# Half of the first 1024 tokens of x turned on TensorE instead of by transposing loads

## The chip, the cores and the metric

The kernel runs on one core of one Trainium2 chip. The metric is device time in microseconds. The kernel before took 833.27 us (median of 4 runs, 832.85 to 833.89). One execution was profiled; it took 833.1 us, and its trace spans 831.4 us from the first to the last instruction, so 1.7 us of it lie outside the trace.

## The reference, cut to what matters

The input x has 2048 tokens of 512 bf16 values. Two blocks work on the same x and are mixed token by token:

```python
g = sigmoid((x * gate_w).sum(-1))
q, k, v = split(x @ wqkv)                 # 32 heads of 16 columns each
o = softmax(q @ k.T / 4) @ v              # per head, 2048 x 2048 scores
a = o @ wo
b = (silu(x @ w_gate) * (x @ w_up)) @ w_down   # hidden width 1792
out = g * a + (1 - g) * b
```

Most of the work is the exponential of 32 x 2048 x 2048 scores.

## The kernel before, in words

**Tiling.** The tokens lie in 4 query blocks of 512 (QBW) and 16 key tiles of 128 (KT). Four heads form a group, and there are 8 groups. A unit is one query block with one group; there are 32 units, each with 16 key tiles. The order of units (UNIT, line 115) takes group 0 of all four query blocks first. For each unit and key tile TensorE makes four score tiles of 128 x 512. Two of them share one PSUM tile `s_t`, and ScalarE turns it into `e_t` with one exponential of 128 x 1024 (`emit_pair`, line 709). Some key tiles go to VectorE instead: `emit_d` (line 742) makes the scores one at a time in `d_t`, and VectorE builds the exponential in steps (`y_t`, `z_t`, `u_t`), with one accumulating DMA from GpSimd's queue (line 789) and a last VectorE step when that has landed (`last`, line 792). Both kinds are then multiplied with V on TensorE (`o_ps`, line 876).

**Order.** The order of instructions on each engine is fixed when the program is built. `ordered` (line 146) chains every TensorE, ScalarE, VectorE and SP-queue instruction issued after it is defined to the one before on its engine. A planner (`Plan`, line 281, and the loop at line 1372) keeps model clocks `plan.pe`, `plan.dve` and `plan.act` and decides from them which piece comes next: a score pair, a score tile for VectorE, a product with V, or a piece of a side chain. Side chains (projections, gate, feed-forward) have a release slot and a due slot. A change of one model clock at the start can therefore move any later instruction, although none is added or dropped.

**Transposed input.** Every projection needs x with its 512 columns on the partitions. The tile is `xT[128, 4, 2048]`: index `dc` says which 128 columns. Lines 177 to 179 fill it with eight transposing loads on SP's queue, four (`dc` 0 to 3) for tokens 0 to 1023 and then four for tokens 1024 to 2047. Behind them on the same queue stand the rest of the V weights (line 190, tile `rb`), the rest of the Q and K weights (line 192), `gw_col`, `wo_t` and `wo_l`. ScalarE's queue loads the 64 columns of K, Q and V that group 0 needs (lines 183 and 188).

**Start.** VectorE clears small tiles, copies the K and then the Q columns of group 0 into padded weights `wpad` (line 234), and writes ones into `kaug` for groups 1 to 3 (`ones_rows`, lines 237 to 241). GpSimd clears and fills constants; `ident`, the identity matrix, is made at lines 268 to 271. TensorE runs 14 matmuls on zeros (`keep_warm`, line 996), and then for each `dc` two matmuls into `kp0` (K of the first 1024 tokens), one into `qp0` (Q of the first 512), and two more on zeros between (lines 1019 to 1026). After these come, in order: the largest magnitude of K on VectorE (`largest`), the bound `kneg1`, its product on TensorE (`bound_add`), the two query variants `q0a` on VectorE (line 1034), and with them the first scores and the first exponential. ScalarE writes `kaug` for group 0 from `kp0` (line 1030) and evicts V of group 0 (`v0`, line 454). VectorE then writes ones for group 4 (line 1037). Line 1045 sets the planner's VectorE clock to `plan.pe + 3.0`. K of the second 1024 tokens follows as side chains (`k0_pieces`, line 1052), with the bounds over all keys (`bound_all`, line 1063) and the query block computed again (`again`, line 1091).

**End.** After the last exponential TensorE adds up the last output projections. `tail` (line 969) issues the five matmuls of each of two row blocks, one group of five before the last product with V (line 1434) and one after it (line 1452). Then follow the copy `osb`, the denominators (`dt`, `rt`, `rps`), the scaling `on_l`, four matmuls, four evictions and the stores (lines 1453 to 1477).

**Tiles that are shared.** `wd_t` (line 198) holds the feed-forward's last weights later; until they are loaded, from slot 88 on (line 1264), VectorE uses its first four rows as a work buffer (line 765). `ps_s` has two PSUM tiles of two banks for `kp0` and the `s_t`; `ps_m` has three single banks, handed out by `m_tile` (line 340).

Of the kernel before, what the change touches and what calls it, by code (L numbers as in the profile page):

```python
# [8 lines left out]
ACT = mybir.ActivationFunctionType  # L9
ALU = mybir.AluOpType  # L10
AX = mybir.AxisListType
BF16 = mybir.dt.bfloat16
F32 = mybir.dt.float32
# [66 lines left out]
def kernel(  # L80
# [12 lines left out]
    nc = tc.nc  # L93
    P = 128
    x = A_x.flatten_outer_dims()
    S, D = x.shape
# [5 lines left out]
    DC = D // P  # L102
    FC = F // P
    KT = S // P
    QBW = 512
    QB = S // QBW
    TQ = QBW // P
# [23 lines left out]
    const = ctx.enter_context(tc.tile_pool(name="const", bufs=1))  # L131
    big = ctx.enter_context(tc.tile_pool(name="big", bufs=1))
# [6 lines left out]
    ps_s = ctx.enter_context(tc.tile_pool(name="ps_s", bufs=2, space=bass.MemoryType.PSUM))  # L139
# [6 lines left out]
    def ordered(ins):  # L146
        i = ins.ins
        if i.engine in last_of:
            tc.add_manual_dep(
                i, last_of[i.engine].name,  # L150
                mybir.DependencyInfo(mybir.DependencyClass.NoSync, mybir.DependencyReason.DATA),
                reason="order",
            )
        last_of[i.engine] = i
        return ins

    def mm(*args, **kw):
        return ordered(nc.tensor.matmul(*args, **kw))  # L158

    def act(*args, **kw):  # L160
        ordered(nc.scalar.activation(*args, **kw))  # L161
# [10 lines left out]
    vec = Ordered(nc.vector)  # L172
    queue = Ordered(nc.sync)


    xT = big.tile([P, DC, S], BF16, name="xT")
    for t0 in (0, 2 * QBW):
        for dc in range(DC):
            queue.dma_start_transpose(out=xT[:, dc, t0:t0 + 2 * QBW], in_=x[t0:t0 + 2 * QBW, dc * P:(dc + 1) * P])
    wqk = big.tile([P, DC, 2 * D], BF16, name="wqk")  # L180
    for c0 in (D, 0):

        nc.scalar.dma_start(out=wqk[:, :, c0:c0 + 64],
                            in_=A_wqkv[:, c0:c0 + 64].rearrange("(dc p) c -> p dc c", p=P))

    rb = big.tile([P, NB, QBW], BF16, name="rb")
    wv = rb[:, :, :]
    nc.scalar.dma_start(out=wv[:, :, 0:64], in_=A_wqkv[:, 2 * D:2 * D + 64].rearrange("(dc p) c -> p dc c", p=P))
# [2 lines left out]
    for c0 in (D, 0):  # L191
        queue.dma_start(out=wqk[:, :, c0 + 64:c0 + D],
                          in_=A_wqkv[:, c0 + 64:c0 + D].rearrange("(dc p) c -> p dc c", p=P))
# [1 line left out]
    wo_t = big.tile([P, NB, D], BF16, name="wo_t")  # L195

    wo_l = big.tile([P, 2, D], BF16, name="wo_l")
    wd_t = big.tile([P, FC, D], BF16, name="wd_t")

    def late_loads():  # L200
        queue.dma_start(out=gw_col[:], in_=gate_w.rearrange("(dc p) -> p dc", p=P))
# [10 lines left out]
    kaug = big.tile([P, G, S], BF16, name="kaug")  # L212
# [4 lines left out]
    wpad = [mt[:, i, :].rearrange("p (dc c) -> p dc c", c=P) for i in range(2)]  # L217
# [12 lines left out]
    nc.vector.memset(bsel0, 0.0)  # L230
    for j in range(4):
        nc.vector.memset(bsel0[32 * j:32 * j + 32, 32 * j:32 * j + 1], -1.0)
    for i in (1, 0):
        nc.vector.tensor_copy(
            out=wpad[i][:, :, :].rearrange("p dc (j c) -> p dc j c", c=32)[:, :, :, 1:1 + DH],
            in_=wqk[:, :, i * D:i * D + 64].rearrange("p dc (j c) -> p dc j c", c=DH))
    def ones_rows(engine, g):

        engine.memset(kaug[:, g, :].bitcast(F32), 1.0019378662109375)
    for g in range(1, 4):  # L240
        ones_rows(nc.vector, g)
    vaug = big.tile([P, KT, G * 4 * VC + 16], BF16, name="vaug")
    nc.gpsimd.memset(vaug[:, :, G * 4 * VC:], 0.0)

# [20 lines left out]
    nc.gpsimd.memset(sel_t[:], 0.0)  # L265
    for j in range(4):
        nc.gpsimd.memset(sel_t[32 * j:32 * j + 1, j:j + 1], 1.0)
    ident = const.tile([P, P], BF16, name="ident")
    nc.gpsimd.memset(ident[:], 1.0)
    nc.gpsimd.affine_select(out=ident[:], in_=ident[:], pattern=[[-1, P]], compare_op=ALU.is_equal,  # L270
                            fill=0.0, base=0, channel_multiplier=1)

    kb = const.tile([P, NB], F32, name="kb")
    kneg = const.tile([P, NB, 8], BF16, name="kneg")
# [13 lines left out]
    plan = Plan()  # L288
# [38 lines left out]
    def m_ready(n=1):  # L327

        t = sorted(b for b in banks if b is not None)
        return t[n - 1] if len(t) >= n else None  # L330

    def stuck():
        if d_wait:
            pay_d()
        elif owed:
            pay()
        else:
            emit_piece(pace.cur)

    def m_tile(name):  # L340
        while m_ready() is None:
            stuck()
        i = min((i for i in range(3) if banks[i] is not None), key=lambda i: banks[i])
        plan.pe = max(plan.pe, banks[i])
        banks[i] = None
        held[i] = ps_m[i].tile([P, QBW], F32, tag=f"m{i}", name=name)
        return held[i]

    def m_free(ps, t):
        i = [h is ps for h in held].index(True)  # L350
        banks[i], held[i] = t + 0.2, None
# [152 lines left out]
    for g in range(5, G):  # L504
        ones_rows(nc.gpsimd, g)
# [487 lines left out]
    qp0 = m_tile("qp0")  # L993
    warm = ps_o.tile([P, QBW], F32, tag="o", name="warm")

    def keep_warm(n):
        for _ in range(n):
            mm(warm[:, :], lhsT=idle[:, 0:P], rhs=idle[:, :], start=True, stop=True)
# [14 lines left out]
    def largest(i, ps):  # L1013
        vec.tensor_reduce(out=kpart0[:, i:i + 1], in_=ps, axis=AX.X, op=ALU.max, apply_absolute_value=True)
# [1 line left out]
    def k_neg(to, i, before):  # L1016
        vec.scalar_tensor_tensor(out=to, in0=bsel0, scalar=kpart0[:, i:i + 1], in1=before, op0=ALU.mult, op1=ALU.min)

    keep_warm(14)
    for dc in range(DC):  # L1020
        for tb in range(2):
            mm(kp0[:, tb * QBW:(tb + 1) * QBW], lhsT=wpad[1][:, dc, :], rhs=xT[:, dc, tb * QBW:(tb + 1) * QBW],
               start=(dc == 0), stop=(dc == DC - 1))
        mm(qp0[:, :], lhsT=wpad[0][:, dc, :], rhs=xT[:, dc, 0:QBW], start=(dc == 0), stop=(dc == DC - 1))
        if dc < DC - 1:
            keep_warm(2)
    largest(0, kp0[:, :])
    k_neg(kneg1, 0, idle[:, 0:P])
    act(out=aq0, in_=qp0[:, :], func=ACT.Abs)
# [4 lines left out]
        vec.tensor_scalar(out=q0a[:, v, :], in0=qp0[:, :], scalar1=vsel[:, v:v + 1], scalar2=None, op0=ALU.mult)  # L1034
    vec.tensor_copy(out=q0_bf[0], in_=qp0[:, :])
    m_free(qp0, plan.pe + 2.0)
    ones_rows(vec, 4)

    vec.tensor_scalar(out=lo_t[:], in0=lo_t[:], scalar1=pidx[:, 0:1], scalar2=None, op0=ALU.subtract)
    vec.tensor_scalar(out=far_t[:], in0=lo_t[:], scalar1=-float(DH) + 0.5, scalar2=-1.0,  # L1040
# [1 line left out]
    vec.scalar_tensor_tensor(out=bsel[:, :], in0=lo_t[:], scalar=0.5, in1=far_t[:],  # L1042
                                   op0=ALU.is_lt, op1=ALU.mult)
    plan.act = plan.pe
    plan.dve = plan.pe + 3.0


    pace = Pacer()
# [60 lines left out]
    for qb in range(1, QB):  # L1109
        d = qb * KT  # L1110
# [5 lines left out]
    for qb in range(QB):  # L1116
        for b in range(NB):
            d = UNIT.index((qb, max(2 * b, 1))) * KT
# [253 lines left out]
    while au < UNITS:  # L1372
# [10 lines left out]
        if room > 0.02:  # L1383
# [19 lines left out]
            if room > 0.4 and closed in o_of and 0 < pvs[closed] < KT - 1 and (closed or pvs[0] != KT // 2) and sum(  # L1403
                    w for t, w in work_at[-24:] if t > plan.pe - 3.0) < 6.5:

                for j in range(4):
                    mm(o_of[closed][32 * j:32 * j + 16, :], lhsT=vaug[:, 0, G * 4 * VC:], rhs=xT[:, 0, 0:QBW],
                       start=False, stop=False, tile_position=(0, 32 * j), skip_group_check=True)
# [50 lines left out]
    for tq in range(TQ):  # L1459
        for j in range(4):  # L1460
            mm(rps[32 * j:32 * j + 32, tq * P:(tq + 1) * P],
               lhsT=rt[:, 4 * tq + j:4 * tq + j + 1].broadcast_to([P, 32]), rhs=ident[:, :],
               start=True, stop=True, tile_position=(0, 32 * j), skip_group_check=True)
# [45 lines left out]
```

## Time and profile before

| what | value |
|---|---|
| time, median of 4 runs | 833.27 us |
| the profiled execution, its own time | 833.1 us |
| its span in the trace | 831.4 us |
| busy in the span: ScalarE, VectorE, TensorE | 810.0, 797.1, 788.3 us |
| exponentials on ScalarE | 844, 788.7 us, mean 1106 ns |
| first exponential starts, last one ends | 13.91 us, 821.72 us |
| score tiles on VectorE | 360 (90 groups of four) |

A line of the timeline gives the start, the busy time, the engine, the source line, the operation, what is written and read (partitions x elements, type), how many were merged, and in brackets how long the engine stood idle before it and what ended that. Lines 158, 161 and 170 are helpers through which TensorE, ScalarE and VectorE (and SP's queue) instructions are recorded, so the tiles' names tell them apart. "SPq" and "ACTq" are the queues that issue DMAs: their times are times of issue, not of transfer. Consecutive instructions on one engine overlap a little, so a mean of 1106 ns goes with a shorter distance from one start to the next.

### The profile page before, as it was taken

What the parts mean: (1) busy time and instruction counts of PE and PEld (TensorE: products, weight loads), DVE (VectorE), ACT (ScalarE), POOL (GpSimd) and SP (SyncE); (2) the same over time, 40 slices, a digit from 0 to 9 for tenths busy, and PEclk for the clock granted to TensorE, in tenths of its full rate; (3) what the DMA queues carried; (4) which work ended last, traced back from release to release, by engine and by line L of the source; (5) the groups of instructions that cost most, each with busy time, mean ns of one, the idle gap of its engine ahead of it and who ended that gap; (6) DMA issues with size and microseconds to landing.
All of it is one profiled execution on the core that took longest, in us unless ns stands there. A gap on an engine that the chain in (4) does not pass through costs nothing. (4 is left out here: it accounts for less than half of the span.)

```text
span 831.4 us, 20368 instructions
## 1 busy us (share of the span) xinstructions
PE 788.3 (95%) x8111; PEld 233.9 (28%) x8111; DVE 797.1 (96%) x1175; ACT 810.0 (97%) x908; POOL 103.0 (12%) x124
## 2 busy tenths in 40 slices
PE   8999999999999999999999999999999899989996
PEld 3322332222232222222232222222222222222222
DVE  6899999999999999999999999999999999999995
ACT  4999999999999999999999999999999999999996
POOL 5001101000001111101011101001011001111000
PEclk9999999999999999999999999999999999999999
DMA  9123336485454354545343563534344644633424
GB/s 206 30 52 65 66 71 121 88 182 102 104 116 84 69 103 109 110 106 113 80 83 62 118 135 83 124 83 85 78 84 93 116 111 91 121 78 77 83 48 99
DMA packets 101719, 79.54 MB, mean 96 GB/s; under 512 B 77792, under 2 KB 89656, under 8 KB 101624
## 3 DMA queue, kind: packets, MB, share of 16 engines
q0 software_dynamic: 12960, 47.19, 30.1%
q1 hardware_dynamic: 86792, 30.60, 15.8%
q8 instruction: 63, 1.03, 0.5%
q10 hardware_dynamic: 1872, 0.46, 0.2%
q14 instruction: 32, 0.26, 0.1%
HBM read 20.83 MB, written 2.34 MB: 28 GB/s over the span
## 5 line engine op out<-in xcount | busy, mean ns | idle before, releaser
L161 ACT ACTIVATE e_t<-s_t 128x1024 bf16<-128x1024 f32 x844 | 788.7, 1106 | 3.2 <-PE s_t L158 2.0
L158 PE MATMUL s_t<-qx,kaug 64*128 64x512 bf16 x1344 | 276.8, 383 | 22.4 <-ACT e_t L161 20.4
L170 DVE TENSOR_SCALAR y_t<-d_t 128x512 uint16<-128x512 f32 x360 | 235.2, 682 | 4.0 <-PE d_t L158 3.6
L158 PEld LDWEIGHTS <-kaug 64*128 64x128 bf16 x2048 | 110.8, 93 | 334.3 <-issue 323.9
L158 PE MATMUL o_ps<-e_t,vaug 128*32 128x512 bf16 x1688 | 169.3, 390 | 0.5 <-ACT e_t L161 0.2
L158 PE MATMUL d_t<-qx,kaug 64*128 64x512 bf16 x288 | 100.8, 380 | 3.2 <-DVE y_t L170 1.2
L158 PEld LDWEIGHTS <-vaug 128*32 128x32 bf16 x2064 | 51.8, 93 | 129.9 <-issue 128.2
L789 POOL DMA_DIRECT2D y_t<-u_t x45 | 45.9, 1020 | 330.4 <-PE s_t L158 166.2
L789 POOL DMA_DIRECT2D y_t<-kaug x39 | 39.3, 1009 | 313.2 <-PE s_t L158 196.0
L158 PE MATMUL gu<-xT,wg 128*32 128x512 bf16 x896 | 76.9, 383 | 0.4 <-DVE gs L170 0.3
L158 PE MATMUL dps<-wd_t,mt 128*32 128x512 bf16 x896 | 76.7, 383 | 0.3 <-DVE y_t L170 0.3
L158 PE MATMUL gu<-xT,wu 128*32 128x512 bf16 x896 | 72.3, 382 | 0.1
L170 DVE TENSOR_SCALAR y_t<-y_t 128x2048 uint16<-128x2048 uint16 x90 | 61.6, 684 | 6.0 <-DMA y_t<-u_t 4.1
L170 DVE TENSOR_SCALAR z_t<-y_t 128x2048 uint16<-128x2048 uint16 x90 | 61.9, 688 | 1.3
L170 DVE TENSOR_TENSOR u_t<-u_t 128x2048 f16<-128x2048 f16 x45 | 54.9, 1221 | 0.8
L170 DVE TENSOR_TENSOR u_t<-u_t,z_t 128x2048 f16<-128x2048 f16 x45 | 54.7, 1215 | 0.1
L170 DVE TENSOR_TENSOR kaug<-kaug 128x2048 f16<-128x2048 f16 x39 | 47.5, 1218 | 0.8
L170 DVE TENSOR_TENSOR kaug<-kaug,z_t 128x2048 f16<-128x2048 f16 x39 | 47.4, 1216 | 0.2
L158 PE MATMUL s_t<-q,kaug 64*128 64x512 bf16 x204 | 42.1, 383 | 4.9 <-ACT e_t L161 4.5
L170 DVE SCALAR_TENSOR_TENSOR mt<-gs,gu 128x512 bf16<-128x512 bf16 x56 | 38.2, 683 | 2.5
L170 DVE SCALAR_TENSOR_TENSOR gs<-th,gu 128x512 bf16<-128x512 bf16 x56 | 37.9, 676 | 0.4 <-ACT th L161 0.3
L161 ACT ACTIVATE th<-gu 128x512 bf16<-128x512 f32 x56 | 38.1, 680 | 0.0
(129 smaller groups left out, 557.3 us busy)
## 6 DMA issues: line engine op xcount, KB each, us to landing
y_t<-u_t POOLq DMA_DIRECT2D x45, 512.0 KB, 5.1
y_t<-kaug POOLq DMA_DIRECT2D x39, 512.0 KB, 5.0
wg<-in_B_w_gate_dram SPq DMA_DIRECT2D x56, 128.0 KB
wu<-in_B_w_up_dram SPq DMA_DIRECT2D x56, 128.0 KB
y_t<-wd_t POOLq DMA_DIRECT2D x6, 512.0 KB, 5.0
on<-osb SPq DMA_DIRECT2D x120, 16.0 KB
rb<-rr SPq DMA_DIRECT2D x15, 128.0 KB
wd_t<-in_B_w_down_dram SPq DMA_DIRECT2D x7, 256.0 KB
```

The lines of the kernel that those rows point to most:

```text
L158: return ordered(nc.tensor.matmul(*args, **kw))
L161: ordered(nc.scalar.activation(*args, **kw))
L170: return lambda *a, **kw: ordered(f(*a, **kw))
L789: nc.gpsimd.dma_start(out=ya, in_=ua, accum_op=ALU.add)
```

## The change

For tokens 0 to 1023 only columns 0 to 255 (`dc` 0 and 1) are still loaded transposed. Columns 256 to 511 come with one plain load on ScalarE's queue, third in it, into the first four rows of `wd_t` (named `x_rows`, eight blocks of 128 tokens x 256 columns). TensorE turns them with 16 matmuls of 128 x 128 against `ident`: `dc` 3 into a two-bank `ps_s` tile that ScalarE evicts with one copy of 128 x 1024, and `dc` 2 into two `ps_m` banks that VectorE evicts with two copies of 128 x 512. The four transposing loads of tokens 1024 to 2047 stay. Matmuls on zeros go from 14 + 6 to 11 + 1 + 3. The projections take `dc` in the order 0, 2, 3, 1. `ident` is made first on GpSimd. The ones for groups 1 and 2 are written before the two `wpad` copies, and those for group 3 move behind the start, ahead of group 4. The planner's VectorE clock starts 0.9 later.

```diff
     xT = big.tile([P, DC, S], BF16, name="xT")
+    wd_t = big.tile([P, FC, D], BF16, name="wd_t")
+    HALF = DC // 2
+    x_rows = wd_t[:, 0:4, :].rearrange("p f d -> p (f d)").rearrange("p (i d) -> p i d", d=HALF * P)
     for t0 in (0, 2 * QBW):
-        for dc in range(DC):
+        for dc in range(DC if t0 else HALF):
             queue.dma_start_transpose(out=xT[:, dc, t0:t0 + 2 * QBW], in_=x[t0:t0 + 2 * QBW, dc * P:(dc + 1) * P])
...
+    nc.scalar.dma_start(out=x_rows, in_=x[0:2 * QBW, HALF * P:D].rearrange("(i p) d -> p i d", p=P))
     rb = big.tile([P, NB, QBW], BF16, name="rb")
...
     for i in (1, 0):
+        ones_rows(nc.vector, 2 - i)
         nc.vector.tensor_copy(
...
-    for g in range(1, 4):
-        ones_rows(nc.vector, g)
+    ident = const.tile([P, P], BF16, name="ident")
+    nc.gpsimd.memset(ident[:], 1.0)
+    nc.gpsimd.affine_select(out=ident[:], in_=ident[:], pattern=[[-1, P]], compare_op=ALU.is_equal,
+                            fill=0.0, base=0, channel_multiplier=1)
...
-    keep_warm(14)
-    for dc in range(DC):
+    def turn(dc, ps):
+        for k in range(2 * TQ):
+            mm(ps[k // TQ][:, k % TQ * P:(k % TQ + 1) * P], lhsT=x_rows[:, k, (dc - HALF) * P:(dc - HALF + 1) * P],
+               rhs=ident[:, :], start=True, stop=True)
+
+    keep_warm(11)
+    tp = ps_s.tile([P, 2 * QBW], F32, tag="s", name="tp")
+    turn(DC - 1, [tp[:, 0:QBW], tp[:, QBW:2 * QBW]])
+    act(out=xT[:, DC - 1, 0:2 * QBW], in_=tp[:, :], func=ACT.Copy)
+    tps = [m_tile("tp") for _ in range(2)]
+    turn(DC - 2, tps)
+    for k in range(2):
+        vec.tensor_copy(out=xT[:, DC - 2, k * QBW:(k + 1) * QBW], in_=tps[k][:, :])
+        m_free(tps[k], 0.0)
+    keep_warm(1)
+    arrived = (0, 2, 3, 1)
+    for dc in arrived:
         for tb in range(2):
             mm(kp0[:, tb * QBW:(tb + 1) * QBW], lhsT=wpad[1][:, dc, :], rhs=xT[:, dc, tb * QBW:(tb + 1) * QBW],
-               start=(dc == 0), stop=(dc == DC - 1))
-        mm(qp0[:, :], lhsT=wpad[0][:, dc, :], rhs=xT[:, dc, 0:QBW], start=(dc == 0), stop=(dc == DC - 1))
-        if dc < DC - 1:
-            keep_warm(2)
+               start=(dc == arrived[0]), stop=(dc == arrived[-1]))
+        mm(qp0[:, :], lhsT=wpad[0][:, dc, :], rhs=xT[:, dc, 0:QBW], start=(dc == arrived[0]), stop=(dc == arrived[-1]))
+        if dc != arrived[-1]:
+            keep_warm(1)
...
-    ones_rows(vec, 4)
+    for g in (3, 4):
+        ones_rows(vec, g)
...
-    plan.dve = plan.pe + 3.0
+    plan.dve = plan.pe + 3.9
```

More of the change, by code (lines that the diff above doesn't have):

```diff
@@ L197 @@
     wo_l = big.tile([P, 2, D], BF16, name="wo_l")
-    wd_t = big.tile([P, FC, D], BF16, name="wd_t")
     def late_loads():
@@ L232, with ones_rows @@
         nc.vector.memset(bsel0[32 * j:32 * j + 32, 32 * j:32 * j + 1], -1.0)
+    def ones_rows(engine, g):
+        engine.memset(kaug[:, g, :].bitcast(F32), 1.0019378662109375)
     for i in (1, 0):
+        ones_rows(nc.vector, 2 - i)
         nc.vector.tensor_copy(
@@ L236 @@
             in_=wqk[:, :, i * D:i * D + 64].rearrange("p dc (j c) -> p dc j c", c=DH))
-    def ones_rows(engine, g):
-        engine.memset(kaug[:, g, :].bitcast(F32), 1.0019378662109375)
-    for g in range(1, 4):
-        ones_rows(nc.vector, g)
+    ident = const.tile([P, P], BF16, name="ident")
+    nc.gpsimd.memset(ident[:], 1.0)
+    nc.gpsimd.affine_select(out=ident[:], in_=ident[:], pattern=[[-1, P]], compare_op=ALU.is_equal,
+                            fill=0.0, base=0, channel_multiplier=1)
     vaug = big.tile([P, KT, G * 4 * VC + 16], BF16, name="vaug")
@@ L267 @@
         nc.gpsimd.memset(sel_t[32 * j:32 * j + 1, j:j + 1], 1.0)
[L268 to L271, printed above, removed]
     kb = const.tile([P, NB], F32, name="kb")
```

## The prediction

> **What bounds the kernel now.** I read the page's busy shares first, then three stretches cut at the first and the last exponential, and then the timeline of both ends.
>
> The stretches (columns: length, then busy time and instructions of each engine, granted clock, DMA share, GB/s):
>
> ```profile
> 0.00:13.90 13.90, 11.13 (x70) 5.00 (x70) 7.90 (x27) 3.48 (x4) 10.90 (x34) 1.00 0.95 170
> 13.90:821.70 807.80, 772.56 (x8001) 227.03 (x8002) 785.37 (x1140) 805.11 (x902) 92.10 (x90) 1.00 0.46 95
> 821.70:831.40 9.70, 4.62 (x40) 1.87 (x39) 3.85 (x9) 1.39 (x3) 0.00 (x0) 0.86 0.16 54
> ```
>
> In the middle ScalarE works 805.1 of 807.8 us: it is the bound, with 2.7 us idle in all. So the profiled time is a sum: 13.9 before the first exponential + 807.8 + 9.7 after the last + 1.7 outside the trace = 833.1 us (0.2 below the median of the four runs). The change can win at the start, in ScalarE's 2.7 idle us, or at the end. "Same" below means within 0.2% of 833.27, about what a measurement of this kernel can tell from no change: 831.6 to 834.9 us.
>
> The start, TensorE and VectorE:
>
> ```profile
> 1.26 5.52 PE L158 MATMUL warm<-mt 128*128 128x512 bf16 x14 [1.26 <-DVE mt L216]
> 6.62 0.59 PE L158 MATMUL kp<-xT,mt 128*128 128x512 bf16 x2
> ...
> 9.85 0.59 PE L158 MATMUL kp<-xT,mt 128*128 128x512 bf16 x2
> ...
> 5.80 0.91 DVE L239 MEMSET kaug<- 128x1024 f32 x1
> ...
> 10.48 1.23 DVE L170 TENSOR_REDUCE kpart<-kp 128x1 f32<-128x1024 f32 x1 [1.63 <-PE kp L158]
> ...
> 14.85 0.91 DVE L170 MEMSET kaug<- 128x1024 f32 x1 [0.16 <-issue]
> ...
> 21.75 0.69 DVE L170 CAST mt<-qp 128x512 bf16<-128x512 f32 x1 [1.76 <-PE qp L158]
> ```
>
> TensorE has no gap from 1.26 to 10.5: no bracket stands at any `kp`. The trace's semaphore records give the landings of the first four transposing loads: 5.64, 6.61, 7.54, 8.97 us. Their matmuls start at 6.62, 7.70, 8.77, 9.85, so each lies ready 0.9 to 1.2 us. **The loads that the change removes do not set the start today; the zeros ahead of the projections do.** The last `kp` ends at 10.44, and 3.47 us later the first exponential starts.
>
> The end:
>
> ```profile
> 821.77 0.39 PE L158 MATMUL o_ps<-e_t,vaug 128*32 128x512 bf16 x2 [0.25 <-ACT e_t L161]
> 822.10 0.82 PE L158 MATMUL al<-wo_t,on 128*128 128x512 bf16 x3
> ...
> 823.28 0.40 PE L158 MATMUL o_ps<-y_t,vaug 128*32 128x512 bf16 x4
> ...
> 822.05 0.69 DVE L170 TENSOR_SCALAR y_t<-y_t 128x2048 uint16<-128x2048 uint16 x1 [3.09 <-DMA y_t<-u_t]
> 823.73 0.69 DVE L170 CAST osb<-o_ps 128x512 bf16<-128x512 f32 x1 [0.98 <-PE o_ps L158]
> ```
>
> VectorE's last exponential is ready at 822.74, 1.0 us after ScalarE's. TensorE meanwhile does five `al` matmuls, and only at 823.28 the last product that `osb` needs. The end is set by that order.
>
> [...] 512 columns take 0.427 us each until 5.92, 0.216 after; the clock record turns full at 6.0. [...] the second load on ScalarE's queue, issued by 1.82, has its first data at 3.62, as the first transposing load (2.42 to 3.89) drains. [...]
>
> **The change part by part.**
>
> *Landing of the plain load.* It takes the place of the third load on ScalarE's queue, whose data ran from 3.99. It has 1024 packets of 512 B, 64 per DMA engine. Packet records give 18 ns at 256 B and 41 at 896 B; between them I estimate 27 ns at 512 B, so 1.7 us. The transposing loads need 1.3 us for a nominal 64 x 18 ns = 1.15; at that efficiency the plain load ends at 5.95 alone, and at 7.2 if the second transposing load (data from 4.12) takes every other turn. From last data to semaphore took 0.7 (second transposing load) to 1.2 us (third ScalarE load). So it lands between 6.6 and 8.4; a perfect case gives 6.2. I take **6.9**, since it is queued ahead of the second transposing load.
>
> *From there to the end of the projections.* The 11 zeros end at 1.26 + 11 x 0.427 = 5.95, so TensorE waits about 1 us. Then 16 turns x 56 ns = 0.9, one zero 0.22, `dc` 0 three matmuls 0.65, a zero 0.22: 2.0 us after landing. VectorE's first copy can begin 0.9 after landing (12 turns and a matmul's 0.22 us of latency) and the two take 0.68 + 0.60 (as the CASTs above): done at 2.2. So `dc` 2's second matmul waits 0.02 and goes at 2.22; `dc` 2 and 3 end at 3.3, a zero at 3.5, and the last `kp` ends at 3.51 + 0.22 + 0.38 = 4.1. ScalarE's copy [...] is done at 1.8, hidden, in its idle 7.0 us before 10.70. The two transposing loads that are gone bring nothing here, since no matmul waited for them. Sum: 6.9 + 4.1 = 11.0 against 10.44: **+0.6 us**; from -0.1 (landing 6.2) to +2.1 (8.4).
>
> *What costs nothing, and its cover.* The second transposing load lands by 8.6 even if it shares; it is used at 10.4. The 64 columns of V come last on ScalarE's queue (landing 5.86 today, perhaps 8.5), used after 11; without that cover their delay would count in full. `ident` on GpSimd (0.2 + 0.3) moves first; its other fills move later by 0.5, and their first reader is `o_ps` at 17.1. The ones for groups 1 and 2 (0.91 each) fill VectorE's waits for the weight loads: the K copy goes at 3.85 instead of 3.38, its reader is past 7. `tp` takes the second `s_t` buffer, so the first score waits for ScalarE's read of `kp0`; it needs `kaug` from that same instruction anyway. VectorE's work buffer in `wd_t` is first written at 27.6, long after the turns. SP's queue: two issues of 1.3 us less, so the weight loads behind (landing 16.98 to 19.37) come about 1 us sooner; nothing waited for them (first V piece at 17.72), so no gain.
>
> *The ones for group 3* add 0.91 to VectorE after 14.85, ahead of the second half of K. Behind it are the K bounds and then `qp`; VectorE idles 1.76 before 21.75, which covers it. Without that cover the first `d_t` would slip 0.9, not the exponentials.
>
> *The later planner clock* changes the order on every engine. Both built programs have 844 exponentials, 56 tanh and 360 `d_t`, so the 807.8 us have the same content. New stalls can at most spoil or save a part of the 2.7 idle us: 0, within 0.7 either way.
>
> *The end.* In the changed program TensorE has VectorE's last product ahead of ScalarE's last one; only one group of five `al` stands between. Is VectorE ready? Before, 22 score pairs follow the last `d_t`; now 23, so its chain starts 0.9 us earlier against ScalarE. Behind the last `d_t` VectorE also has one product of 128 x 2048 (`u_t` by `z_t`, 1.2) less: ready about 2.1 us earlier, at 1.1 before the last exponential's end instead of 1.0 after. The last `o_ps` then goes at about 0.45 after that end instead of 1.55 (823.28 against 821.73): **-1.1 us**, 0 if VectorE is a microsecond late. I take -0.9.
>
> Sum: 833.1 + 0.6 + 0 - 0.9 = **832.8 us**, a gain too small to measure.
>
> **The rivals.**
> *Slower: TensorE starts the projections cold.* Place: between the last zero at 5.95 and the landing. [...] if the release is missed, the 16 turns cost 0.8 more and 15 matmuls of 512 columns 0.21 more each, 3.2: [...] +2.8 in a typical miss: 835.6. It decides if the clock is not full by about 9 us. For it: the zeros cover only 4.7 us, and the release came at 6.0. Against: TensorE is busy without a gap for 4.7 us first[...].
> *Faster: everything lines up.* Landing 6.2 (-0.1), end -1.1, stalls -0.7: 831.2. For it: ScalarE's waits of 0.24 and 0.48 us at 16.1 and 24.0 sit where the order changes. Against: no load holds the start today.
> *It does nothing at the end.* VectorE's last step comes late, +0.6 remains: 833.7.
>
> **How the numbers follow.** Forecast 0.45 and nothing-at-the-end 0.15 are within 0.2%: same 0.60. Faster 0.20 (831.2), slower 0.20 (835.6). The range, 831.0 to 835.6, reaches to both outer cases and leaves out about one in ten at each side.
>
> **What would show it.** First `tp` matmul at 6.9 with a DMA as releaser; last `kp` end near 11.0 and first exponential near 14.5; full clock before 7; middle stretch 807.8 within 0.7; last exponential to last instruction 8.8 instead of 9.7. A landing past 8.4, a clock record past 9, or a middle stretch off by over a microsecond proves it wrong.

## The result: 0.2% slower, with a late and cold start that the later planner clock half pays back

| | before | after |
|---|---|---|
| time, median (lowest to highest) | 833.52 us (832.06 to 836.27) of 58 runs | 835.62 us (833.62 to 837.19) of 39 runs |
| ratio of the two, 95% interval | | 1.0021, 1.0017 to 1.0026 |
| profiled execution, its own time | 833.1 us | 835.62 us |
| its span in the trace | 831.4 us | 833.9 us |
| last `kp` matmul ends | 10.45 us | 15.38 us |
| first exponential starts, last one ends | 13.91, 821.72 us | 18.86, 825.07 us |

It is slower by 0.21%, a difference that is small but clear of no change, and the forecast of 832.8 us, no measurable change, was wrong. The three stretches of the changed kernel (length; busy time and instructions of TensorE, its weight loads, VectorE, ScalarE, GpSimd; granted clock, DMA share, GB/s):

```profile
0.00:18.86 18.86, 13.99 (x81) 6.54 (x81) 9.04 (x28) 4.51 (x6) 11.18 (x34) 1.00 0.94 195
18.86:825.07 806.21, 771.07 (x8002) 226.77 (x8003) 784.90 (x1142) 804.42 (x902) 91.39 (x90) 1.00 0.46 93
825.07:833.90 8.83, 3.82 (x37) 1.54 (x35) 3.15 (x8) 1.38 (x3) 0.00 (x0) 0.97 0.18 59
```

Against the kernel before: start +4.95 us, middle -1.6, end -0.8, together +2.5. The start alone would have cost 5 us. ScalarE does the same 902 instructions in the middle; its idle time there falls from 2.7 to 1.8 us and its busy time by 0.7.

The start (timeline):

```profile
1.26 4.88 PE L158 MATMUL warm<-mt 128*128 128x512 bf16 x11 [1.26 <-DVE mt L219]
...
8.20 1.89 PE L158 MATMUL tp<-ident,wd_t 128*128 128x128 bf16 x16 [2.07 <-DMA wd_t<-in_A_x_dram]
...
9.28 1.02 ACT L161 ACTIVATE xT<-tp 128x1024 bf16<-128x1024 f32 x1 [4.93 <-PE tp L158]
...
9.70 1.29 DVE L170 CAST xT<-tp 128x512 bf16<-128x512 f32 x2 [3.16 <-PE tp L158]
...
10.31 1.06 PE L158 MATMUL kp<-xT,mt 128*128 128x512 bf16 x2
...
13.72 0.79 PE L158 MATMUL kp<-xT,mt 128*128 128x512 bf16 x2
...
14.79 0.59 PE L158 MATMUL kp<-xT,mt 128*128 128x512 bf16 x2
...
18.86 1.94 ACT L161 ACTIVATE e_t<-s_t 128x1024 bf16<-128x1024 f32 x2 [0.57 <-PE s_t L158]
```

Two things stand here. The turns begin at 8.20, after 2.07 us in which TensorE waits for the plain load. And everything then runs at half speed: 16 turns in 1.89 us (1.07 in a kernel below where the clock is full), two `kp` in 1.06. The pair at 13.72 is the first to speed up within itself; the next takes the 0.59 us that every pair took before. The trace's clock record turns full at 14.1, against 6.0 in the kernel before. (The granted clock of the first two stretches reads 1.00: the half clock ahead of the first record isn't counted there. The duration of one `qp` matmul shows it: 0.63 us at 11.16, 0.38 at 14.36.)

The end:

```profile
822.67 0.69 DVE L170 TENSOR_SCALAR y_t<-y_t 128x2048 uint16<-128x2048 uint16 x1 [2.81 <-DMA y_t<-u_t]
...
824.27 0.40 PE L158 MATMUL o_ps<-y_t,vaug 128*32 128x512 bf16 x4
...
824.60 0.82 PE L158 MATMUL al<-wo_t,on 128*128 128x512 bf16 x3
...
825.78 0.40 PE L158 MATMUL o_ps<-e_t,vaug 128*32 128x512 bf16 x4
...
826.24 0.69 DVE L170 CAST osb<-o_ps 128x512 bf16<-128x512 f32 x1 [2.88 <-PE o_ps L158]
```

VectorE's last step is done at 823.36, 1.7 us before the last exponential's end instead of 1.0 after it. Its product goes at 824.27, and ScalarE's product is the last, 0.71 us after the exponential's end, where before the last product went 1.55 us after it.

### The profile page after: what moved, and what is told of

Read it like the earlier page. It is cut to its first block, busy times and chain, and to the rows that moved or that the text cites. A ratio compares the mean times of both kernels' runs of the same rounds, so it can differ in the third digit from the quotient of the medians.

```text
span 833.9 us, 20394 instructions
## 1 busy us (share of the span) xinstructions
PE 788.9 (95%) x8118; PEld 234.8 (28%) x8118; DVE 797.1 (96%) x1177; ACT 810.3 (97%) x909; POOL 102.6 (12%) x124
## 5 line engine op out<-in xcount | busy, mean ns | idle before, releaser
L161 ACT ACTIVATE e_t<-s_t 128x1024 bf16<-128x1024 f32 x844 | 788.1, 1105 | 2.4 <-PE s_t L158 1.6
L158 PE MATMUL s_t<-qx,kaug 64*128 64x512 bf16 x1336 | 273.7, 383 | 25.4 <-ACT e_t L161 22.1
L158 PEld LDWEIGHTS <-vaug 128*32 128x32 bf16 (+1 forms) x2060 | 50.7, 93 | 122.7 <-issue 121.6
```

## The experiments

The theory after this comparison: (a) the plain load lands late, and the gap that it leaves in TensorE's work makes TensorE miss the release of its clock; (b) the planner's later VectorE clock, not the loads, earns what the middle and the end give back. The rivals: the late landing alone explains the start; the middle is shorter only because it starts later; the turns themselves, with their evictions, are the cost. Every ratio is against the kernel before, run alongside on the same chip.

### The new order without the turned half

The changed kernel with its eight transposing loads back and no turns:

```diff
-        for dc in range(DC if t0 else HALF):
+        for dc in range(DC):
-    nc.scalar.dma_start(out=x_rows, in_=x[0:2 * QBW, HALF * P:D].rearrange("(i p) d -> p i d", p=P))
-    keep_warm(11)
...
-    keep_warm(1)
-    arrived = (0, 2, 3, 1)
+    keep_warm(14)
+    banks[1] = banks[2] = 0.2
+    arrived = (0, 1, 2, 3)
-            keep_warm(1)
+            keep_warm(2)
```

The line with `banks` tells the planner that two PSUM banks come free when they do in the changed kernel, so that its choices stay the same.

> The eight transposing loads and the zeros (14, and 2 between) of the kernel before, with the later planner clock and the moved ones of the changed kernel, so that every engine's order after the start is the changed kernel's. If the new order alone gave the 1.6 us less in the middle and the 0.9 us less at the end: first exponential at 13.9, middle 806.2, end 8.8, with 1.7 outside the trace 830.6 us. If the shorter middle was only the other side of the late start (stalls that happen anyway before 18.9 us): middle 807.8 and about 832.2 with the shorter end, or 833.1 without it.

Measured: 830.22 us (829.79 to 832.07), ratio 0.9962 (0.9948 to 0.9976). The stretches:

```profile
0.00:14.23 14.23, 11.43 (x70) 5.06 (x70) 7.76 (x26) 3.48 (x5) 11.17 (x34) 1.00 0.93 167
14.23:819.30 805.07, 770.82 (x8001) 226.92 (x8003) 784.72 (x1142) 803.73 (x902) 91.81 (x90) 1.00 0.46 95
819.30:828.10 8.80, 3.81 (x36) 1.53 (x35) 3.15 (x8) 1.37 (x2) 0.00 (x0) 0.87 0.18 60
```

With a start like that of before, the middle is 2.7 us and the end 0.9 us shorter. So the gain doesn't come from the loads, nor from a later start: this kernel starts its exponentials 0.3 us after the kernel before. The profiled execution was the fastest of the seven, so its 2.7 us is a favourable reading; the median time is 0.38% down, about 3.2 us. The turned half costs about 5 us on top of it.

### The planner's clock alone

The kernel before with one number changed:

```diff
-    plan.dve = plan.pe + 3.0
+    plan.dve = plan.pe + 3.9
```

> The kernel before with one number changed: the planner's VectorE clock starts at 3.9 instead of 3.0. TensorE, ScalarE and SP's queue then have exactly the order of e1_order_only; VectorE differs only in the place of the ones for group 3. If the order is what gained: first exponential 13.9, middle 805 to 806, end 8.8, 830.2 us as e1_order_only. If the ones' later place on VectorE is needed for it: slower than 831.

Measured: 830.14 us (828.92 to 831.37), ratio 0.9955 (0.9942 to 0.9967). One number accounts for the whole gain of the new order; where the ones are written and when `ident` is made add nothing that can be seen in the times. Its profiled execution was the slowest of its five (831.37): there the end is 8.8 us, but the middle 807.16, with the clock record dropping at 14.4 and full again at 17.8 (12 `kp` matmuls of 32 columns of weights take 1.35 us from 14.26 on, where 20 took 1.26 in the kernel before), and 1.7 of ScalarE's 3.0 us of idling between 15.6 and 18.4. So the shorter middle of this kernel rests on its times and on the profile of the kernel above, not on its own profile.

### Zeros until the load has landed

The changed kernel with `keep_warm(20)` for `keep_warm(11)`.

> The changed kernel with 20 matmuls on zeros before the turns in place of 11, so that TensorE is busy until the plain load lands near 8.2. If the start was lost to TensorE's half clock: full clock at 6 to 8 us, first exponential at 8.2 + 4.1 + 3.5 = 15.8, 832.5 us, some 3 us better than the changed kernel. If it was lost to the landing and to the turns and evictions behind it: unchanged at 835.6.

Measured: 832.54 us (831.45 to 833.86), ratio 0.9986 (0.9979 to 0.9993). TensorE:

```profile
1.25 6.33 PE L158 MATMUL warm<-mt 128*128 128x512 bf16 x20 [1.25 <-DVE mt L219]
8.32 1.07 PE L158 MATMUL tp<-ident,wd_t 128*128 128x128 bf16 x16 [0.74 <-DMA wd_t<-in_A_x_dram]
...
9.44 0.59 PE L158 MATMUL kp<-xT,mt 128*128 128x512 bf16 x2
...
12.05 0.38 PE L158 MATMUL kp<-xT,mt 128*128 128x512 bf16 x1
```

The load lands at 8.27, as late as in the changed kernel (8.16), yet the last `kp` ends 3 us earlier: 4.16 us after the landing instead of 7.22. The clock record is full at 5.0. So a late landing alone does not explain the start. Nine more matmuls on zeros are worth 3 us, and the turns, warm, cost what the forecast said (4.1). With these zeros the change is 0.14% faster than the kernel before, but it is still 2.3 us behind the new order without turns: its first exponential starts at 16.11 instead of 14.23. That part goes with the landing at 8.27, which the zeros don't change.

### A gap without turned loads

The kernel before with `keep_warm(6)`, and with `keep_warm(4)`, for `keep_warm(14)`: the gap alone, no load or order changed.

> The kernel before with 6 matmuls on zeros ahead of the projections in place of 14: they end at 3.8, and TensorE idles until the first transposing load lands at 5.6. No turn and no plain load is in it. If idle time before the projections costs the release of the clock: clock full past 9 us, last kp near 13 instead of 10.4, 835 to 836 us. If the clock is not what costs the time: last kp at 10 or earlier, 833 us or a little less.

> The kernel before with 4 zeros in place of 14: they end near 3.0, [...] the projections cannot begin before 5.6. If an unbroken busy window is what releases the clock: no release before 8.5 in any execution, projections at half clock, last kp past 12, 836 us or more in the median and in the profiled run. If the release follows the total of busy time or the start of the program: clock full near 6, last kp at 10, 833 us.

Measured with six: 835.6 us (833.25 to 837.67), ratio 1.0019 (1.0011 to 1.0028). Its profiled execution was the fastest of its 22, with the clock full by the first `kp` (two in 0.59 us at 5.55), so its trace does not show the cost that the median has. With the clock full, eight zeros fewer end the last `kp` at 9.81 instead of 10.45: the zeros that the prediction names as setting the start cost 0.6 us here, since the first `kp` then waits for VectorE's copy of the weights. With four: 835.58 us (834.58 to 836.76), ratio 1.0019 (1.0010 to 1.0028), and its trace does show it:

```profile
1.26 1.89 PE L158 MATMUL warm<-mt 128*128 128x512 bf16 x4 [1.26 <-DVE mt L216]
5.73 1.01 PE L158 MATMUL kp<-xT,mt 128*128 128x512 bf16 x2 [2.59 <-DMA xT<-in_A_x_dram]
...
7.82 1.06 PE L158 MATMUL kp<-xT,mt 128*128 128x512 bf16 x2
...
11.12 0.59 PE L158 MATMUL kp<-xT,mt 128*128 128x512 bf16 x2
```

The projections begin 0.9 us earlier than before (5.73 against 6.62) and end 1.3 us later (11.72), cold until the record turns full at 10.1 (the pair at 9.95 takes 0.69 us, 1.06 before). The late release came as expected; the median stayed 0.4 us under the 836 us that were to go with it. A gap ahead of the projections costs about 1.6 us in the median with nothing else changed.

### The load first in its queue

The changed kernel with the plain load ahead of the Q and K weights on ScalarE's queue; and then the same with the Q copy moved to ScalarE:

```diff
-        nc.vector.tensor_copy(
-            out=wpad[i][:, :, :].rearrange("p dc (j c) -> p dc j c", c=32)[:, :, :, 1:1 + DH],
-            in_=wqk[:, :, i * D:i * D + 64].rearrange("p dc (j c) -> p dc j c", c=DH))
+        to = wpad[i][:, :, :].rearrange("p dc (j c) -> p dc j c", c=32)[:, :, :, 1:1 + DH]
+        of = wqk[:, :, i * D:i * D + 64].rearrange("p dc (j c) -> p dc j c", c=DH)
+        if i:
+            nc.vector.tensor_copy(out=to, in_=of)
+        else:
+            nc.scalar.activation(out=to, in_=of, func=ACT.Copy)
```

> The changed kernel with the plain load first on ScalarE's queue instead of third. If the landing sets the start: it lands near 6, hardly any idle time before the turns, clock full by about 6 to 9, first exponential near 14, 831 us. If the half clock comes from the turns rather than from the idle time: first exponential near 17, 834 us. The two small weight loads come later; if their copies are the last thing waited for, the first kp shows a wait for VectorE.

> e3_load_first with the second wpad copy (the Q columns) on ScalarE instead of VectorE. In e3 that VectorE copy took 3.85 us, until GpSimd had finished its fills at 12.0. If GpSimd's fills held up VectorE's copy: the copy on ScalarE takes under 0.6 us, qp follows kp without the 4.2 us gap, last kp near 11 instead of 16.6, first exponential near 14.5, 831 to 832 us. If the late landing of the Q columns (7.6 us) was the cause, with VectorE merely waiting for it: a gap of several us remains and 836 us.

Measured: load first, 837.47 us (836.96 to 837.67), ratio 1.0042 (1.0029 to 1.0056), slower still: neither of the two times expected came true, and a wait for VectorE shows, at the first `qp`. The load lands at 5.47 and the turns run warm at 5.92, but:

```profile
5.92 1.20 PE L158 MATMUL tp<-ident,wd_t 128*128 128x128 bf16 x16
...
7.54 1.81 POOL L505 MEMSET qx<- 128x2048 bf16 x1
...
8.27 3.85 DVE L241 COPY mt<-wqk 128x256 bf16<-128x256 bf16 x1
...
9.28 2.74 POOL L238 MEMSET kaug<- 128x1024 f32 x3
...
12.18 0.39 PE L158 MATMUL qp<-xT,mt 128*128 128x512 bf16 x1 [4.21 <-DVE xT L170]
```

The Q copy takes 3.85 us on VectorE (the K copy of the same shape, at 7.05, took 0.26) and ends at 12.12, just after GpSimd's fills at 12.02. TensorE idles 4.21 us; the clock record drops at 13.0, so the matmuls that follow are cold again until 16.4. With that copy on ScalarE, 832.47 us (830.91 to 833.77), ratio 0.9985 (0.9977 to 0.9993):

```profile
7.72 1.28 ACT L246 ACT_TABLE_LOAD   x1 [7.72 <-DMA wqk<-in_A_wqkv_dram]
...
9.02 0.45 ACT L246 ACTIVATE mt<-wqk 128x256 bf16<-128x256 bf16 x1
...
9.52 0.39 PE L158 MATMUL qp<-xT,mt 128*128 128x512 bf16 x1 [1.57 <-ACT mt L246]
```

That is 5 us better, for a copy of 0.45 us on another engine: the landing of the Q columns, which the expectation names as the other cause, was not what held the copy. But the Q weights, now behind the plain load, come at about 7.7, and the table load stands behind the same wait. So `qp` still waits 1.57 us, the last `kp` ends at 12.28 and not near 11, and the first exponential starts at 15.76, 1.5 us after the 14.23 of the new order without turns. With the load third or first in its queue, the turned half is later than the transposing loads that it replaces.

### Three zeros fewer

The new order without turns, with `keep_warm(11)` for `keep_warm(14)`.

> e1_order_only with 11 zeros ahead of the projections in place of 14. The first transposing load lands at 5.6 and the 11 zeros end at 5.95, so no gap opens and the release of the clock is not touched: projections start up to 0.7 us earlier (three zeros at 0.22), then wait for the later loads at 6.6, 7.5 and 9.0, so the last kp ends near 9.8: 829.6 us. If three zeros are within the noise of the release: 830.2.

Measured: 831.02 us (829.76 to 831.84), ratio 0.9961 (0.9949 to 0.9974), the same as with 14 within the intervals. The reason is on VectorE:

```profile
6.56 0.61 PE L158 MATMUL kp<-xT,mt 128*128 128x512 bf16 x2 [0.43 <-DVE kaug L237]
```

The zeros end at 6.13, and the first `kp` waits 0.43 us more, for VectorE, which has a fill and the copy of the K columns to do in the changed kernel's order. There that copy took 2.45 us and ended at 6.46, where it took 0.53 in the kernel before; the last section comes back to it. So the projections could not start 0.7 us earlier, and of the two readings expected it is the second, no gain.

### Is 3.9 a good number for a late start too?

The kernel before with all of x loaded plainly and turned on TensorE, a start 12 us longer; then the planner's clock at 3.0, 3.9, 4.8 and 3.45:

```diff
-    for t0 in (0, 2 * QBW):
-        for dc in range(DC):
-            queue.dma_start_transpose(out=xT[:, dc, t0:t0 + 2 * QBW], in_=x[t0:t0 + 2 * QBW, dc * P:(dc + 1) * P])
+    for to, t0, t1 in ((wd_t[:, 0:8, :], 0, 8), (wd_t[:, 8:14, :], 8, 14), (bblk[:, 0:2, :], 14, 16)):
+        queue.dma_start(out=to, in_=x[t0 * P:t1 * P, :].rearrange("(i p) d -> p i d", p=P))
...
     keep_warm(14)
+    for h in range(2):
+        for dc in range(DC):
...
+            for k in range(2 * TQ):
+                mm(ps[k // TQ][:, k % TQ * P:(k % TQ + 1) * P], lhsT=x_row(8 * h + k)[:, dc * P:(dc + 1) * P],
+                   rhs=ident[:, :], start=True, stop=True)
```

> A third start, the same in four kernels: all of x comes with plain loads and is turned on TensorE before the projections (64 turns into each half, no transposing load), so the first exponential comes late, some 22 to 26 us. Behind it this kernel has the order of the kernel before (planner's VectorE clock 3.0). If the order sets the middle and the end whatever the start: middle 807.8 within 1, end 9.65. If a late start shortens the middle: 805 to 806.

> The same start with the changed kernel's order (clock 3.9). If the order sets them: middle 805 to 806.3, end 8.8, and 2.5 to 3.5 us less than with clock 3.0. If the order is not the cause: the same time as with clock 3.0.

> The same start with clock 4.8: 846 exponentials on ScalarE and 356 score tiles on VectorE in place of 844 and 360. If a later clock is better because it is truer to VectorE: as good as 3.9 or better. If 3.9 is one good order among many: the two further exponentials alone cost 1.8 us of middle, so 1 to 4 us slower than 3.9.

> The same start with clock 3.45, half way. Counts as with 3.0, but the last score tile for VectorE is taken 11 pairs before the end instead of 22. If a later clock is better by itself: between 3.0 and 3.9. If the end follows from where the last VectorE tile falls: end longer than 9.65 and slower than 3.0.

| clock | median us | ratio, 95% | middle of the profile | end |
|---|---|---|---|---|
| 3.0 | 849.97 | 1.0204 (1.0189 to 1.0219) | 812.40 | 9.9 |
| 3.45 | 845.43 | 1.0149 (1.0132 to 1.0166) | 809.36 | 9.3 |
| 3.9 | 843.60 | 1.0128 (1.0113 to 1.0143) | 807.39 | 9.1 |
| 4.8 | 847.58 | 1.0174 (1.0159 to 1.0189) | 810.95 | 8.7 |

ScalarE's waits for its scores, with 3.0 (waited for: us in total, times, longest):

```profile
ACT e_t L161 <- PE s_t L158: 7.2, 12, 2.4
```

and with 3.9:

```profile
ACT e_t L161 <- PE s_t L158: 2.9, 8, 0.9
```

A later start doesn't shorten the middle: with the old clock it is longer than in any other kernel here, and longer than the 807.8 that I expected. At the same late start 3.9 is worth 6.4 us, more than the 2.5 to 3.5 expected, but mostly not for the reason of the earlier kernels. In the profile with 3.0 one place makes up the whole difference of 5.0 us in the middle: between 140.4 and 152.5 us ScalarE idles 5.1 of its 7.7 us. TensorE waits there for a DMA of queries (`qx`, 2.86 us), then the clock record drops at 145.2 and is full again at 152.0 (the mean granted clock of that execution is 0.990, with 3.9 it is 0.995). The kernel before, with the same order of instructions and an earlier start, has no such stall. Nor are the times monotone: 4.8 is worse than 3.9, and 3.45, whose end I expected to be longer than 9.65, lies between 3.0 and 3.9 with 9.3. Of four numbers tried, 3.9 is the best, in an order that changes as a whole each time. The changed kernel itself with the old clock was not measured.

## Why the prediction was wrong

*Landing, taken as 6.9; it was 8.16.* Inside its bounds (6.6 to 8.4), at the wrong end. The packets' 27 ns were nearly right (median 29), and the last data came 0.6 us ahead of the semaphore. The failed step is "I take 6.9, since it is queued ahead of the second transposing load": the place in the queue did not give it the engines. Of its 1024 packets about 900 were through at 6.1; the rest came between packets of the second transposing load until 7.58. Cost +1.26 us.

*From the landing to the last `kp`, 4.1; it was 7.22.* The working was right for a warm TensorE (4.16 in the kernel with 20 zeros) and wrong for this one: +3.1 us. Its 56 ns a turn, which no trace of the kernel before shows, holds with the clock full: with 20 zeros the 16 turns take the 0.90 us from 8.32 to 9.22. In the changed kernel they take the 1.68 us from 8.20 to 9.88, 0.8 more, as the rival says. The step that failed is the case against that rival: with 4.7 us of zeros first, about 1 us of waiting was not to cost the clock. The gap was 2.07 us, since the landing was late, and the record turned full only at 14.12. Three stretches of 3.4 us ahead of that:

```profile
3.88:7.29 3.41, 2.25 (x6) 0.52 (x4) 2.66 (x4) 0.46 (x1) 3.17 (x9) 1.00 1.19 210
7.29:10.70 3.41, 2.50 (x18) 1.99 (x19) 1.00 (x2) 1.02 (x1) 3.27 (x6) 1.00 1.29 223
10.70:14.12 3.42, 3.42 (x9) 1.21 (x8) 0.29 (x1) 0.00 (x0) 1.50 (x2) 1.00 1.15 204
```

TensorE (second number) idles 1.16 us in the first and 0.91 in the second; in the third it has no gap, and at its end the record turns full. That TensorE was busy without a gap first (here 4.88 us of zeros) did not help. Nor do the traces give one length of work that brings the full clock: behind the same 14 zeros from 1.26 us on it came at 6.0 in the kernel before and at about 4.2 with the clock alone, where the 14 took 4.62 us instead of 5.52. In the two executions profiled, six zeros (2.74 us) and a gap of 1.55 us left the next matmuls at full clock, four (1.89 us) and a gap of 2.59 us at half. How much idle time the full clock bears is not shown; that 1 us would do no harm was my estimate.

Only one execution of the changed kernel was profiled. It lies on the median time, but most others took another way to it. Each execution has its mean granted clock on record, in which half clock ahead of the first release isn't counted. The half clock at the end of the trace takes 0.2% of it at most (before, changed kernel, new order without turns, clock alone, and all of x turned with 3.0 and 3.9), so I read 0.997 or less as a clock that was full and was lost again. That holds for 27 of the changed kernel's 39 executions (the profiled one reads 1.00), for 8 of 22 with 20 zeros, and for 6 of 44 of the kernel before that ran alongside. Where in the execution these others lost it is not shown.

*The middle, 807.8 within 0.7; it was 806.2.* The failed step is "The later planner clock ... 0, within 0.7 either way". The same instructions were taken to mean the same time, and the stalls to matter by a part of 2.7 us. Of the 1.6 us, 0.9 is less idling, and 0.7 less busy time for the same exponentials (788.7 to 788.1 us). That busy time holds waits too. Exponentials that follow each other directly start 0.90 us apart and last 1.11, and the overlap counts once, so a start up to 0.2 us late shows as busy time. Counted from the starts, such lateness, whatever it comes from, comes to 12.0 us in the kernel before (135 starts), 10.9 in the changed kernel (118) and 10.7 in the new order without turns (121). So the 2.7 us of idling were not all that another order could save. In the five other kernels with the new order and a start like these the middle was 804.9 to 806.4, against 807.8 to 808.6 in the three with the old one, the clock-only profile (807.16) apart. Which change of place in the order brings the earlier starts stays open.

*The end, -0.9; it was -0.8.* Right in reason and nearly in size: the order of the last products, with VectorE ready first. The kernel with the clock alone has it too (8.8).

*The covers* held: no new wait shows between the last `kp` and the first exponential, 3.48 us against 3.47. One was needed more than forecast: the copy of the K columns, taken to be 0.5 us later, ended 2.5 us later (6.46 instead of 3.91), which the landing at 8.16 hid.

*The signs.* Of the three that were to prove it wrong, two came: the clock record past 9 us (14.1) and the middle off by over a microsecond (1.6). The landing stayed under 8.4.

*The sum.* +0.6 + 1.26 + 3.1 - 1.6 - 0.8 = +2.56, and 2.5 was measured. The rival "TensorE starts the projections cold" named the mechanism and even the number (835.6), but partly by luck: its start lacked the 1.3 us of the landing, and its middle the 1.6 us that came back.

The best kernel of the study is the one before with 3.9 for 3.0, 830.14 us, or equally the new order without turns, 830.22.

## What to carry to other kernels

Where TensorE has to be warm for what follows, let the filler run until the slowest plausible landing: here a gap of 2 us cost 3 us, and nine more matmuls on zeros brought them back. A change that bundles a data path with a planner's constant is to be tested apart: the constant alone made the kernel 0.45% faster, and the data path cost 5 us on top. Of a load that shares its DMA engines with others take the late end of its bound when a wait hangs on it.

## What the runs showed of the hardware that I had not expected

A VectorE copy of 128 x 256 bf16 that took 0.26 us for the K columns took 3.85 us for the Q columns beside GpSimd's fills of `qx` and `kaug` (7.54 to 12.02) with the load first, and ended 0.1 us after them; it took 2.74 us in the kernel with all of x turned and clock 3.0 (9.37 to 12.11, GpSimd's fills until 12.00), and the same copy on ScalarE took 0.45. The changed kernel has it too, at its start:

```profile
4.01 2.53 DVE L241 COPY mt<-wqk 128x256 bf16<-128x256 bf16 x2
```

The first of these two copies took 2.45 us and ended at 6.46, 0.1 us after GpSimd's fill of `q` (5.40 to 6.34). These are times side by side; what holds the copy is not shown.

TensorE's clock can be lost again after it was full, and one long gap isn't needed: with the load first it was lost at 13.0, after a gap of 4.21 us, but with the planner's clock alone at 14.4, after gaps of 0.56, 0.94 and 0.27 us that end at 11.94, 13.28 and 13.94. In the kernel before, gaps of 0.55, 0.94 and 0.27 us that end at 12.15, 13.49 and 14.15 lost nothing: its record stays full from 6.0 to 828.6. So the gaps alone do not tell when the clock is lost, and what else decides it is not shown.
